# Sums of v for five blocks a visit beside the sequence transform, two exponential buffers in the projections' home, and one-pass turning of maxima

## The chip, the cores and the metric

The kernel runs on 1 core of one Trainium2 chip. The metric is the time of one execution in device microseconds; the median over the runs is compared.

## The reference

One sequence of 2048 rows of width 512 (x) goes two ways, and a gate for each row mixes the results. The inputs are float32.

```python
g = sigmoid((x * gate_w).sum(-1, keepdims=True))
# A: real part of a Fourier transform, by matrices, over the width and then over the sequence
a, b = x @ Wd_re.T, x @ Wd_im.T
y = Ws_re @ a - Ws_im @ b
# B: attention with 32 heads of width 16 in a causal window of 256
qkv = x @ wqkv
scores = q @ k.T * 16 ** -0.5;  mask = (0 <= i - j) & (i - j < 256)
o = softmax(where(mask, scores, -1e9)) @ v;  b_out = o @ wo
return g * y + (1 - g) * b_out
```

The weights wqkv and wo are scaled up by about 48 and 49, so scores are large and the maxima of the softmax are needed.

## The kernel before, in words

**Dense work.** Every dense product runs as three fp32r matmuls: each operand is split into a rounded part "hi" and the rest "lo", and hi x hi, hi x lo and lo x hi are summed in PSUM. A generator `dense()` yields behind each matmul, so that attention can be put between. It makes in this order: the projections to q and k of head group 0 together with v, then q and k of groups 1 to 3, with the imaginary part b of the width transform behind group 1 and the real part a at the end (`have.add("proj")` then marks that all projections are done), then the sequence transform: 16 blocks with cr, 16 with ci (L446, "dc", 48 matmuls a block), and, in its last blocks, the output projections `wo_block` (L669).

**Homes of the projections.** Results of q, k and part of a and b are evicted in split form into a tile "hl" (`split_psum`: ScalarE writes hi, VectorE writes lo) and sent to DRAM (qk_scr, ab_scr) by one 512 KB transfer of SP's queue. The tile hl has three buffers. Nothing uses it in the sequence transform.

**Attention.** There are 4 groups of heads with 32 blocks of 64 positions each, so 128 blocks, and 4 pairs of heads in a group. In round n, `s_pair` (L325) makes the scores of block n as a query block, VectorE adds the mask and takes the maximum (L327), and ScalarE takes the exponential and its row sum (L330); only maximum and sum are kept, in "ml". In the same round `t_pair` (L388) makes the transposed scores of block k = n - 20 as a key block, with the queries' maxima as an extra row of the operand in the ring, and ScalarE writes the exponentials into a tile "pt" (L389); GpSimd clears its corners (L394, L398). `pv` (L415) sums v times pt of one block into PSUM, with four 32-column parts of TensorE's array side by side; these are float32 matmuls, of which each makes two records. When eight blocks of 64 are complete, VectorE divides by the sums and SP stores them (o_scr).

**Visits.** `pv` is called at p = 2 of every third round, for three blocks; "pt" has four buffers. v of four blocks is loaded (`v_load`, "vr") and spread by GpSimd into "vpad" (`v_spread`, L378), two sets in turn, by rounds counted in fours.

**Maxima.** After eight blocks, `ml_rows` takes the reciprocal of the sums, turns the 128 x 64 tile of maxima and sums by a float32 matmul with a unit matrix (L337, two records), splits the maxima (L340, L341), copies the sums (L344), and sends them to m_scr and l_scr. It is called behind a visit. `m_ring` loads the maxima back into the ring by ScalarE's queue two or more rounds later.

**Order.** TensorE's order is as written (a manual schedule); `fill` puts 3 to 3.6 dense matmuls beside each pair. The other engines are ordered by a scheduler; `behind(e)` holds an instruction back until the last marked one of engine e is issued. SP's queue issues its transfers in order, so one that waits holds up those behind it. Scores and turned scores and turned maxima share four PSUM tiles.

Of the kernel before, what the change touches and what calls it, by code (L numbers as in the profile page):

```python
# [7 lines left out]
F32 = mybir.dt.float32  # L8
F32R = mybir.dt.float32r
AF = mybir.ActivationFunctionType  # L10
OP = mybir.AluOpType
# [3 lines left out]
P = 128  # L15
# [4 lines left out]
NP = 4  # L20
BQ = 64
NB = S // BQ
WIN = 320
BIG = 1e30
SCALE = 0.25
LAG = 20
# [6 lines left out]
def fnet_window_mix(ctx: ExitStack, tc: tile.TileContext, xT, x, wqk, wv, wr, wi, cr, ci, wo, gw, out):  # L33
    nc = tc.nc

    const = ctx.enter_context(tc.tile_pool(name="const", bufs=1))
    big = ctx.enter_context(tc.tile_pool(name="big", bufs=16))
    st = ctx.enter_context(tc.tile_pool(name="st", bufs=3))
# [16 lines left out]
    def ld(dst, src):  # L55
        mark("sp", nc.sync.dma_start(dst, src))

    def f(ap):
        return ap.bitcast(F32)
# [91 lines left out]
    for h in (0, 64):  # L151
# [2 lines left out]
                                base=0, channel_multiplier=-1)  # L154
        nc.gpsimd.affine_select(m, m, pattern=[[-1, WIN]], compare_op=OP.is_ge, fill=BIG,
                                base=256, channel_multiplier=1)
    ident = const.tile([P, P], F32, name="ident")
    nc.gpsimd.memset(ident, 1.0)
    nc.gpsimd.affine_select(ident, ident, pattern=[[1, P]], compare_op=OP.is_equal, fill=0.0,
                            base=0, channel_multiplier=-1)  # L160

    half = const.tile([P, 2], F32, name="half")
# [55 lines left out]
    TERMS = ((0, 0), (0, 1), (1, 0))  # L218


    def qk_evict(g, ss, i, ps):
        hl = ev.tile([P, 2, 512], F32R, name="hl", bufs=3)
        split_psum(hl[:, 0], hl[:, 1], ps, -SCALE if i == 0 else 1.0)
        ld(qk_scr[i][g][ss].rearrange("h x s -> x h s"), f(hl[:]))

# [59 lines left out]
    def ab_proj(i, sb, w, dst=None):  # L285
        ps = ps_d.tile([P, 512], F32, name="dab", tag="d")
        yield from row_proj(sb, w, ps)
        if dst is None:
            hl = ev.tile([P, 2, 512], F32R, name="hl", bufs=3)
            split_psum(hl[:, 0], hl[:, 1], ps, 1.0 if i == 0 else -1.0)  # L290
            ld(ab_scr[i][sb], f(hl[:]))
        else:
            split_psum(dst[:, 0], dst[:, 1], ps)
        yield
# [16 lines left out]
        PAD[i, n] = t  # L311

    ML = {}

    def s_pair(n, p):
        j = n % NB
        u, jj = divmod(n, 8)
        if jj == 0 and p == 0:
# [11 lines left out]
        mark("act", nc.scalar.activation(sm[:, :w], sm[:, :w], AF.Exp, bias=nm[:, c], scale=-1.0,  # L330
                                         accum_out=l[:, c]))

    def ml_rows(u):
        ml = ML.pop(u)
        nc.vector.reciprocal(ml[:, 1], ml[:, 1])
        pt = ps_a.tile([P, 512], F32, name="s", tag="st")
        nc.tensor.matmul(pt[:64, :P], ml.rearrange("p x c -> p (x c)"), ident, start=True, stop=True)  # L337
        hl = at.tile([32, 2, 2, 64], F32R, name="mhl", bufs=1)
        m = pt[:32, :P].rearrange("c (a r) -> c a r", a=2)
        nc.vector.tensor_scalar(hl[:, :, 0], m, -1.0, None, op0=OP.mult)  # L340
        nc.vector.scalar_tensor_tensor(hl[:, :, 1], m, -1.0, f(hl[:, :, 0]), op0=OP.mult, op1=OP.subtract)  # L341
        ld(m_scr[u].rearrange("x p (j r) -> (p j) x r", r=64), f(hl[:]).rearrange("c a h r -> c (a h) r"))
        lt = at.tile([64, P], F32, name="lt", bufs=1)
        nc.vector.tensor_copy(lt[32:64], pt[32:64, :P])  # L344
        for a in range(2):
            ls = l_scr[u]
            ld(bass.AP(tensor=ls.tensor, offset=ls.offset + a * 512, ap=[[1024, NP], [64, 8], [1, 64]]),
               lt[32:64, 64 * a:64 * a + 64])

    def m_ring(u):  # L350
        U = u % 4
        with behind("act"):
            nc.scalar.dma_start(f(ring[0][96:100, :, U * 512:(U + 1) * 512]), m_scr[u])

    OT = {}
    V2 = {}
    PT = {}

    VR = {}

    def v_load(n):
        if n >= NG * NB:
            return
        g, kb = divmod(n, NB)
        raw = at.tile([P, 4, 64], F32, name="vr", bufs=1)
        for h in range(2):
            ld(raw[64 * h:64 * h + 64].rearrange("r (c j) x -> r c j x", j=2),
               v_scr[kb // 4][:, :, h, g, :].rearrange("c (j r) x -> r c j x", r=64))
        VR[n] = raw

    def v_spread(n):
        if n >= NG * NB:
            return
        raw = VR.pop(n)
        v2 = vpad[n // 4 % 2]
        for h in range(2):
            r = slice(64 * h, 64 * h + 64)
            nc.gpsimd.tensor_copy(v2[r, :, :, 16 * h:16 * h + 16], raw[r].rearrange("r j (p d) -> r j p d", d=16))  # L378
        V2[n // 4] = v2

    def t_pair(n, p):
        q0 = n % NB * BQ
        w = min(WIN, S - q0)
        if p == 0:
            PT[n] = at.tile([P, NP, WIN], F32, name="pt", bufs=4)
        pt = PT[n]
        ps = ps_a.tile([P, 512], F32, name="t", tag="st")
        nc.tensor.matmul(ps[:, :w], PAD[1, n][:, p], ring[0][:, p, q0:q0 + w], start=True, stop=True)  # L388
        nc.scalar.activation(pt[:, p, :w], ps[:, :w], AF.Exp, scale=-1.0)  # L389
        if p % 2:  # L390
            ph = slice(p - 1, p + 1)
            for h in (0, 64):
                a = pt[h:h + 64, ph, 0:64]
                nc.gpsimd.affine_select(a, a, pattern=[[0, 2], [1, 64]], compare_op=OP.is_ge, fill=0.0,  # L394
                                        base=0, channel_multiplier=-1)
                if w == WIN:
                    a = pt[h:h + 64, ph, 256:320]
                    nc.gpsimd.affine_select(a, a, pattern=[[0, 2], [-1, 64]], compare_op=OP.is_gt, fill=0.0,  # L398
                                            base=0, channel_multiplier=1)

    def pv(n):
        g, kb = divmod(n, NB)
        v2 = V2[n // 4][:, n % 4]
        pt = PT.pop(n)
        q0 = kb * BQ
        w = min(WIN, S - q0)
        q = q0
        while q < q0 + w:
            sb = q // 512
            e = min(q0 + w, (sb + 1) * 512)  # L410
            first = (g, sb) not in OT
            if first:
                OT[g, sb] = ps_o.tile([P, 512], F32, name="o")
            for p in range(NP):
                nc.tensor.matmul(OT[g, sb][32 * p:32 * p + 32, q - sb * 512:e - sb * 512], v2[:, p],  # L415
                                 pt[:, p, q - q0:e - q0], start=first, stop=kb == 8 * sb + 7,
                                 skip_group_check=True)
# [260 lines left out]
    def need(key):  # L678
        while key not in have:
            next(stream)  # L680
# [22 lines left out]

    ctx.enter_context(tc.manual_schedule(engines={mybir.EngineType.PE}))
    N = NG * NB
    maxima = sent = 0
    taken = []
    need(("qk", 0, 0))
    ring_ahead(0)
    need(("v", 5))  # L710

    for n in range(N + LAG + 2):
        if n in (1, 3, 5):
            for i in range(2):
                clear_rows(1 - i, (n + 1) // 2)
        if n == 7:
            clear_pads()
        k = n - LAG
        ring_ahead(n + 1)
        if -4 <= k < N - 4 and k % 4 == 0:  # L720
            for c in range(2):
                need(("v", (k + 4) % NB // 2 + c))
            with behind(*(("sp",) if k < 4 else ())):
                v_load(k + 4)
        if -4 <= k and k % 4 == 3:
            v_spread(k + 1)
        if n == 0:
            make_pad(0, 0)
        for p in range(NP):
            if n < N:  # L730
                s_pair(n, p)
            fill(n)
            if 0 <= k < N:
                t_pair(k, p)
            if p == 0:
                make_pad(0, n + 1)
                if k >= -1:
                    make_pad(1, k + 1)
            fill(n)
            if p == 2 and sent < maxima and n >= taken[sent] + 2:  # L740
                m_ring(sent)
                sent += 1
            if p == 2 and k % 3 == 0:
                for j in range(k - 3, k):
                    if 0 <= j < N:
                        pv(j)
                if maxima < 16 and n > 8 * maxima + 8:
                    ml_rows(maxima)
                    maxima += 1
                    taken.append(n)  # L750
    attention_done()
    for _ in stream:
        pass
# [44 lines left out]
```

## Time and profile before

| | us |
|---|---|
| median of 3 runs | 869.55 |
| lowest and highest | 868.85, 870.48 |
| the profiled execution | 873.39 |
| its span | 871.3 |

The page of the profile gives busy time by engine (PE is TensorE's matmuls, PEld its loading of weights, DVE VectorE, ACT ScalarE, POOL GpSimd, SP the queue of transfers), the span in 40 slices, the chain that ended last, and the costliest groups of instructions. A row of a timeline gives the start and the duration in us, the engine, the line, the operation, the tiles written and read, the shape and the count; in brackets stands idle time before it and what ended it. The end of a matmul is modelled, so starts are the surer reading.

### The profile page before, as it was taken

The page shows a single profiled execution, that of the slowest core. Times are in us where ns is not written, and L with a number is a line of the kernel's source. Part 1 is how long each engine was busy: PE and PEld are TensorE (multiplying, and loading weights), DVE is VectorE, ACT ScalarE, POOL GpSimd, SP SyncE. Part 2 cuts the span into 40 slices and gives each one's busy share as a digit, 9 for nine tenths or more (in the row PEclk, how much of TensorE's full clock was granted, in tenths as well). Part 3 has the DMA queues.
Part 4 walks back from the last instruction along what each step waited for, and adds up shares of the span by engine and source line. Part 5 has one row for each costly group of instructions (what it writes and reads, how often), then busy time and mean ns, then how long its engine had stood idle before and what let it go on. Part 6 is the DMA issues. An engine that isn't in the chain of part 4 may idle for free.

```text
span 871.3 us, 17146 instructions
## 1 busy us (share of the span) xinstructions
PE 860.5 (99%) x5160; PEld 690.3 (79%) x5160; DVE 611.3 (70%) x1974; ACT 580.9 (67%) x1793; POOL 384.6 (44%) x1067
## 2 busy tenths in 40 slices
PE   8999999999999999999999999999999999999998
PEld 6888778787877778878788887878778787788886
DVE  4588987667878987878787777788876444564431
ACT  4388799888897987878788777877776454111110
POOL 9100054545444756656456566554546665200000
PEclk9999999999999999999999999999999999999999
DMA  6875796464749436644445354599944333485541
GB/s 229 266 226 155 248 262 197 153 214 158 241 158 289 130 105 225 172 130 135 134 131 170 105 163 133 156 349 256 329 148 159 123 118 114 130 263 192 189 145 48
DMA packets 93132, 157.87 MB, mean 181 GB/s; under 512 B 27120, under 2 KB 36080, under 8 KB 93040
## 3 DMA queue, kind: packets, MB, share of 16 engines
q1 hardware_dynamic: 92288, 155.61, 56.5%
q10 hardware_dynamic: 752, 1.18, 0.4%
q8 instruction: 40, 0.66, 0.3%
q14 instruction: 52, 0.43, 0.2%
HBM read 106.69 MB, written 50.07 MB: 180 GB/s over the span
## 4 chain that ended last, share of the span: by engine, by line
PE 92%; DVE 3%; DMA 2%; ACT 1%; issue 1%; SPq 0%; DVEq 0%; ACTq 0%
PE dc L446 40%; PE dab L266 9%; PE s L325 8%; PE o L415 8%; PE dqk L244 8%; PE t L388 8%; PE t L669 5%; PE dv L266 4%; DVE sm L327 1%; PE s L232 1%; DMA raw<-x 1%; ACT sm L330 1%; DMA ring<-qk_scr 1%; PE s L337 1%; DMA pt<-xT 0%
## 5 line engine op out<-in xcount | busy, mean ns | idle before, releaser
L446 PE MATMUL dc<-big,hi 128*128 128x512 f32 x1024 | 355.4, 395 | 0.0
L394 POOL TENSOR_SCALAR_AFFINE_SELECT pt<-pt 64x128 f32<-64x128 f32 x512 | 191.9, 375 | 276.4 <-ACT pt L389 261.2
L330 ACT ACTIVATE sm<-sm,ml 128x320 f32<-128x320 f32 (+4 forms) x512 | 277.3, 543 | 49.4 <-DVE ml L327 48.0
L327 DVE CUSTOM_DVE_ANT_0 sm<-s,mask 128x320 f32<-128x320 f32 (+4 forms) x512 | 230.7, 462 | 82.7 <-PE s L325 62.5
L389 ACT ACTIVATE pt<-t 128x320 f32<-128x320 f32 (+4 forms) x512 | 208.7, 412 | 89.8 <-PE t L388 86.2
L446 PEld LDWEIGHTS dc<-big,hi 128*128 128x128 f32 x1024 | 186.3, 188 | 32.6 <-issue 2.4
L446 PE MATMUL dc<-big,lo 128*128 128x512 f32 x512 | 201.6, 394 | 0.0
L398 POOL TENSOR_SCALAR_AFFINE_SELECT pt<-pt 64x128 f32<-64x128 f32 x448 | 161.9, 361 | 0.1
L325 PE MATMUL s<-ring,pad 128*128 128x320 f32 (+4 forms) x512 | 159.0, 310 | 0.9 <-DVE ml L327 0.5
L388 PE MATMUL t<-ring,pad 128*128 128x320 f32 (+4 forms) x512 | 155.1, 303 | 1.6 <-DVE ml L327 0.9
L310 DVE TENSOR_SCALAR pad<-ring,half 96x256 fp32r<-96x256 f32 x384 | 121.6, 358 | 24.2 <-PE t L388 22.0
L325 PEld LDWEIGHTS s<-ring,pad 128*128 128x128 f32 x512 | 96.0, 188 | 36.6 <-issue 7.4
L388 PEld LDWEIGHTS t<-ring,pad 128*128 128x128 f32 x512 | 96.1, 188 | 21.6 <-DVE ml L327 2.6
L446 PEld LDWEIGHTS dc<-big,lo 128*128 128x128 f32 x512 | 96.3, 188 | 10.6
L81 DVE TENSOR_TENSOR lo<-raw,hi 128x512 fp32r<-128x512 f32 x146 | 99.6, 712 | 1.4 <-PE dc L446 1.3
L330 ACT ACTIVATION_READ_ACCUMULATOR sm<-sm,ml 128x1 f32 x512 | 98.8, 193 | 0.0
L266 PE MATMUL dab<-hi,big 128*128 128x512 f32 x256 | 90.9, 396 | 0.0
L244 PE MATMUL dqk<-big,hi 128*128 128x512 f32 x240 | 86.7, 394 | 0.6 <-DVE hl L86 0.5
L80 DVE CAST hi<-raw 128x512 fp32r<-128x512 f32 x142 | 58.6, 453 | 38.3 <-PE dc L446 37.1
L415 PE MATMUL o<-pt,vpad 128*32 128x320 f32 (+4 forms) x1408 | 73.8, 351 | 0.0
L378 POOL COPY vpad<-vr 64x256 f32<-64x256 f32 x64 | 26.0, 405 | 91.1 <-DMA vr<-v_scr 72.0
L308 ACT ACTIVATE pad<-ring,half 96x256 fp32r<-96x256 f32 x128 | 64.1, 500 | 0.0
(82 smaller groups left out, 780.3 us busy)
## 6 DMA issues: line engine op xcount, KB each, us to landing
qk_scr<-hl SPq DMA_DIRECT2D x32, 512.0 KB
ring<-qk_scr SPq DMA_DIRECT2D x32, 512.0 KB
raw<-cr SPq DMA_DIRECT2D x32, 512.0 KB
raw<-ci SPq DMA_DIRECT2D x32, 512.0 KB
ab_scr<-hl SPq DMA_DIRECT2D x20, 512.0 KB
big<-ab_scr SPq DMA_DIRECT2D x20, 512.0 KB
r_scr<-ev SPq DMA_DIRECT2D x36, 256.0 KB
ev<-r_scr SPq DMA_DIRECT2D x36, 256.0 KB
```

Of the source, the lines that this page charges most:

```text
L244: nc.tensor.matmul(ps, w[a][:, c:c + 128], XT[dk, ss][:, b], start=n == 0, stop=n == 11)
L266: nc.tensor.matmul(ps, XT[dk, ss][:, a, c * 128:(c + 1) * 128], wh[b], start=n == 0, stop=n == 11)
L310: nc.vector.tensor_scalar(dst, src, half[:96, h:h + 1], None, op0=OP.mult)
L325: nc.tensor.matmul(ps[:, :w], PAD[0, n][:, p], ring[1][:, p, k0:k0 + w], start=True, stop=True)
L327: mark("dve", nc.vector.tensor_tensor_reduce(out=sm[:, :w], in0=ps[:, :w], in1=mask[:, WIN - w:], scale=1.0, scalar=3e38, op0=OP.add, op1= ...
L330: mark("act", nc.scalar.activation(sm[:, :w], sm[:, :w], AF.Exp, bias=nm[:, c], scale=-1.0, accum_out=l[:, c]))
L388: nc.tensor.matmul(ps[:, :w], PAD[1, n][:, p], ring[0][:, p, q0:q0 + w], start=True, stop=True)
L389: nc.scalar.activation(pt[:, p, :w], ps[:, :w], AF.Exp, scale=-1.0)
L394: nc.gpsimd.affine_select(a, a, pattern=[[0, 2], [1, 64]], compare_op=OP.is_ge, fill=0.0, base=0, channel_multiplier=-1)
L398: nc.gpsimd.affine_select(a, a, pattern=[[0, 2], [-1, 64]], compare_op=OP.is_gt, fill=0.0, base=0, channel_multiplier=1)
L415: nc.tensor.matmul(OT[g, sb][32 * p:32 * p + 32, q - sb * 512:e - sb * 512], v2[:, p], pt[:, p, q - q0:e - q0], start=first, stop=kb == 8 ...
L446: nc.tensor.matmul(ps, w[a][:, i % 8 * 128:i % 8 * 128 + 128], ab[SC[i]][:, b], start=i == ends[0] and a + b == 0, stop=i == ends[1] and a ...
```

## The change

It does four things.

- `pv` is called when three blocks wait, and, once all projections are done, when five wait; v is loaded and spread by what has been summed, not by rounds.
- "hl" gets two buffers instead of three, each of the size of a "pt" tile. Once the projections are done, two of every six exponential tiles are put there, so that there are six.
- The maxima are turned in two steps: `ml_split` splits maxima and reciprocals on VectorE, `ml_turn` turns both halves by one-pass fp32r matmuls two rounds later, and `ml_rows` adds the halves of the sums. Their rounds are fixed (`TURN`), and they no longer stand behind a visit.
- The loop has one round less.

```diff
+    def hl_tile():
+        t = ev.tile([P, NP, WIN], F32R, name="hl", bufs=2)
+        return t.rearrange("p a b -> p (a b)")[:, :1024].rearrange("p (h s) -> p h s", h=2)
...
-        hl = ev.tile([P, 2, 512], F32R, name="hl", bufs=3)
+        hl = hl_tile()
...
+    def ml_split(u):
+        ml = ML.pop(u).rearrange("p x c -> p (x c)")
+        MH[u] = at.tile([P, 2, NP * 16], F32R, name="mlh", bufs=1)
+        with behind("dve"):
+            nc.vector.reciprocal(ml[:, 32:], ml[:, 32:])
+            nc.vector.tensor_copy(MH[u][:, 0], ml)
+            mark("dve", nc.vector.tensor_sub(MH[u][:, 1], ml, f(MH[u][:, 0])))
+
+    def ml_turn(u):
+        hl = MH.pop(u)
+        MT[u] = ps_a.tile([P, 512], F32, name="s", tag="st")
+        for h in range(2):
+            nc.tensor.matmul(MT[u][:64, h * P:h * P + P], hl[:, h], ident, start=True, stop=True)
+
     def ml_rows(u):
-        ml = ML.pop(u)
-        nc.vector.reciprocal(ml[:, 1], ml[:, 1])
-        pt = ps_a.tile([P, 512], F32, name="s", tag="st")
-        nc.tensor.matmul(pt[:64, :P], ml.rearrange("p x c -> p (x c)"), ident, start=True, stop=True)
-        hl = at.tile([32, 2, 2, 64], F32R, name="mhl", bufs=1)
-        m = pt[:32, :P].rearrange("c (a r) -> c a r", a=2)
-        nc.vector.tensor_scalar(hl[:, :, 0], m, -1.0, None, op0=OP.mult)
-        nc.vector.scalar_tensor_tensor(hl[:, :, 1], m, -1.0, f(hl[:, :, 0]), op0=OP.mult, op1=OP.subtract)
+        pt = MT.pop(u)
+        rows = at.tile([64, 2 * P], F32R, name="mhl", bufs=1)
+        hl = rows[:32].rearrange("c (a h r) -> c a h r", a=2, h=2)
+        lt = f(rows[32:64, :P])
+        m = pt[:32, :2 * P].rearrange("c (h a r) -> c h a r", h=2, a=2)
+        with behind("dve"):
+            nc.vector.tensor_scalar(hl.rearrange("c a h r -> c h a r"), m, -1.0, None, op0=OP.mult)
+            nc.vector.tensor_copy(lt, pt[32:64, :P])
+            mark("dve", nc.vector.tensor_add(lt, pt[32:64, P:2 * P], lt))
...
-            PT[n] = at.tile([P, NP, WIN], F32, name="pt", bufs=4)
+            if "proj" in have:
+                more.append(n)
+            if more and (n - more[0]) % 6 < 2:
+                PT[n] = f(ev.tile([P, NP, WIN], F32R, name="hl", bufs=2)[:])
+            else:
+                PT[n] = at.tile([P, NP, WIN], F32, name="pt", bufs=4)
...
+    TURN = (8, 1, ml_split), (10, 0, ml_turn), (10, 1, ml_rows), (13, 0, m_ring)
...
-    for n in range(N + LAG + 2):
+    for n in range(N + LAG + 1):
...
-            if p == 2 and sent < maxima and n >= taken[sent] + 2:
-                m_ring(sent)
-                sent += 1
-            if p == 2 and k % 3 == 0:
-                for j in range(k - 3, k):
-                    if 0 <= j < N:
-                        pv(j)
-                if maxima < 16 and n > 8 * maxima + 8:
-                    ml_rows(maxima)
-                    maxima += 1
-                    taken.append(n)
+            for at_n, at_p, do in TURN:
+                u, j = divmod(n - at_n, 8)
+                if p == at_p and j == 0 and 0 <= u < 16:
+                    do(u)
+            if p == 2 and (k - summed >= (5 if more else 3) or k == N):
+                for j in range(summed, k):
+                    pv(j)
+                summed = k
+                while 4 * spread - 5 < summed and 4 * spread < N:
+                    v_spread(4 * spread)
+                    spread += 1
+                    v_next(4 * spread)
```

The unit matrix "ident" becomes fp32r.

More of the change, by code (lines that the diff above doesn't have):

```diff
@@ L156, in fnet_window_mix @@
                                 base=256, channel_multiplier=1)
-    ident = const.tile([P, P], F32, name="ident")
-    nc.gpsimd.memset(ident, 1.0)
-    nc.gpsimd.affine_select(ident, ident, pattern=[[1, P]], compare_op=OP.is_equal, fill=0.0,
+    ident = const.tile([P, P], F32R, name="ident")
+    nc.gpsimd.memset(f(ident[:]), 1.0)
+    nc.gpsimd.affine_select(ident[:], f(ident[:]), pattern=[[1, P]], compare_op=OP.is_equal, fill=0.0,
                             base=0, channel_multiplier=-1)
@@ L288, in ab_proj @@
         if dst is None:
-            hl = ev.tile([P, 2, 512], F32R, name="hl", bufs=3)
+            hl = hl_tile()
             split_psum(hl[:, 0], hl[:, 1], ps, 1.0 if i == 0 else -1.0)
@@ L313, in fnet_window_mix @@
     ML = {}
+    MH = {}
+    MT = {}
     def s_pair(n, p):
@@ L331, in s_pair @@
                                          accum_out=l[:, c]))
-    def ml_rows(u):
-        ml = ML.pop(u)
-        nc.vector.reciprocal(ml[:, 1], ml[:, 1])
-        pt = ps_a.tile([P, 512], F32, name="s", tag="st")
-        nc.tensor.matmul(pt[:64, :P], ml.rearrange("p x c -> p (x c)"), ident, start=True, stop=True)
-        hl = at.tile([32, 2, 2, 64], F32R, name="mhl", bufs=1)
-        m = pt[:32, :P].rearrange("c (a r) -> c a r", a=2)
-        nc.vector.tensor_scalar(hl[:, :, 0], m, -1.0, None, op0=OP.mult)
-        nc.vector.scalar_tensor_tensor(hl[:, :, 1], m, -1.0, f(hl[:, :, 0]), op0=OP.mult, op1=OP.subtract)
-        ld(m_scr[u].rearrange("x p (j r) -> (p j) x r", r=64), f(hl[:]).rearrange("c a h r -> c (a h) r"))
-        lt = at.tile([64, P], F32, name="lt", bufs=1)
-        nc.vector.tensor_copy(lt[32:64], pt[32:64, :P])
+    def ml_split(u):
[10 more added lines that the diff above has]
+            nc.tensor.matmul(MT[u][:64, h * P:h * P + P], hl[:, h], ident, start=True, stop=True)
+    def ml_rows(u):
+        pt = MT.pop(u)
[7 more added lines that the diff above has]
+            mark("dve", nc.vector.tensor_add(lt, pt[32:64, P:2 * P], lt))
+        ld(m_scr[u].rearrange("x p (j r) -> (p j) x r", r=64), f(hl).rearrange("c a h r -> c (a h) r"))
         for a in range(2):
@@ L347, in ml_rows @@
             ld(bass.AP(tensor=ls.tensor, offset=ls.offset + a * 512, ap=[[1024, NP], [64, 8], [1, 64]]),
-               lt[32:64, 64 * a:64 * a + 64])
+               lt[:, 64 * a:64 * a + 64])
     def m_ring(u):
@@ L357, in fnet_window_mix @@
     PT = {}
+    more = []
     VR = {}
@@ L705, in fnet_window_mix @@
     N = NG * NB
-    maxima = sent = 0
-    taken = []
+    TURN = (8, 1, ml_split), (10, 0, ml_turn), (10, 1, ml_rows), (13, 0, m_ring)
     need(("qk", 0, 0))
@@ L710, in fnet_window_mix, with v_next @@
     need(("v", 5))
-    for n in range(N + LAG + 2):
+    summed, spread = 0, 2
+    def v_next(n):
+        if n < N:
+            for c in range(2):
+                need(("v", n % NB // 2 + c))
+            with behind(*(("sp",) if n < 8 else ())):
+                v_load(n)
+    for n in range(N + LAG + 1):
         if n in (1, 3, 5):
@@ L719, in fnet_window_mix @@
         ring_ahead(n + 1)
[L720 to L725, printed above, removed]
+        if k in (-4, 0):
+            v_next(k + 4)
+        if k in (-1, 3):
             v_spread(k + 1)
+        if k == 3:
+            v_next(8)
         if n == 0:
```

## The prediction

> **What bounds the kernel now.** I read the page first (busy times, slices, chain), then TensorE's timeline around the sums of v and the turnings, then the queues and ScalarE around the evictions of the projections.
>
> ```profile
> PE 860.5 (99%) x5160; PEld 690.3 (79%) x5160; DVE 611.3 (70%) x1974; ACT 580.9 (67%) x1793; POOL 384.6 (44%) x1067
> PE   8999999999999999999999999999999999999998
> PEclk9999999999999999999999999999999999999999
> PE 92%; DVE 3%; DMA 2%; ACT 1%; issue 1%; SPq 0%; DVEq 0%; ACTq 0%
> ```
>
> TensorE is busy in every slice, at full granted clock, and carries 92% of the chain that ended last. So two things can move the time: TensorE's own work, and new stalls of TensorE. The idle time of the other engines is cover, not a gain.
>
> **Part 1: fewer visits to the sums of v.** One visit, with what stands before and behind it on TensorE (columns: start, duration, line, form, count):
>
> ```profile
> 524.00 0.40 PE L446 MATMUL dc<-big,lo 128*128 128x512 f32 x1
> 524.32 1.83 PE L415 MATMUL o<-pt,vpad 128*32 128x128 f32 x40
> 526.09 0.41 PE L325 MATMUL s<-ring,pad 128*128 128x320 f32 x1
> 526.34 0.40 PE L446 MATMUL dc<-big,hi 128*128 128x512 f32 x1
> 526.57 0.30 PE L388 MATMUL t<-ring,pad 128*128 128x320 f32 x1
> 526.72 0.40 PE L446 MATMUL dc<-big,hi 128*128 128x512 f32 x1
> ...
> 758.84 21.12 PE dc L446 x92
> ```
>
> Durations overlap, so I take differences of starts. An undisturbed 512-wide matmul costs 21.12/92 = 0.23. Before the visit it costs 0.32 (524.00 to 524.32), so 0.09 is lost going in. The visit runs 1.77 (to 526.09). The 320-wide score matmul behind it takes 0.25, while a 320-wide one inside the stream, at 526.57, hands on after 0.15; so 0.10 is lost coming out. How much of the 1.77 is fixed comes from the last, short visit:
>
> ```profile
> 757.99 0.39 PE L446 MATMUL dc<-big,hi 128*128 128x512 f32 x1
> 758.30 0.54 PE L415 MATMUL o<-pt,vpad 128*32 128x128 f32 x16
> 758.77 0.50 PE L446 MATMUL dc<-big,hi 128*128 128x512 f32 x1
> ```
>
> That one sums 192 columns (128 and 64, the last two blocks) in 0.47; the other sums 3 blocks of 320, 960 columns, in 1.77. So a column costs 1.30/768 = 1.69 ns, and 0.47 - 192 x 1.69 ns = 0.15 is fixed. A visit therefore costs 0.09 + 0.15 + 0.10 = 0.34 beyond its columns, whatever it sums.
>
> Visits before: k = 3, 6, ... 129, which is 43. In the changed kernel's order of TensorE instructions there are 14 visits of three blocks (to k = 42), then k = 47, 52, ... 127 and a last one at 128: 14 + 18 = 32. The columns stay. So 11 x 0.34 = **-3.7 us**, all on TensorE and so on the path.
>
> **Part 2: turning the maxima.** Before, 14 of the 16 turnings stand directly behind a visit and two stand alone. A lone one, then one behind a visit:
>
> ```profile
> 96.73 0.39 PE L244 MATMUL dqk<-big,hi 128*128 128x512 f32 x1
> 97.05 0.43 PE L337 MATMUL s<-ident,ml 128*64 128x128 f32 x2
> 97.41 0.41 PE L325 MATMUL s<-ring,pad 128*128 128x320 f32 x1
> 97.66 0.39 PE L244 MATMUL dqk<-big,hi 128*128 128x512 f32 x1
> ...
> 555.16 1.84 PE L415 MATMUL o<-pt,vpad 128*32 128x256 f32 x48
> 556.93 0.43 PE L337 MATMUL s<-ident,ml 128*64 128x128 f32 x2
> 557.29 0.41 PE L325 MATMUL s<-ring,pad 128*128 128x320 f32 x1
> 557.54 0.39 PE L446 MATMUL dc<-big,lo 128*128 128x512 f32 x1
> ...
> 341.45 0.33 PE L325 MATMUL s<-ring,pad 128*128 128x128 f32 x1
> 341.62 0.68 PE L446 MATMUL dc<-big,hi 128*128 128x512 f32 x2
> ```
>
> The lone one costs 0.09 going in, 0.36, and 0.10 coming out: 0.55. Behind a visit it adds only 0.36, since the way out is paid anyway. Before: 14 x 0.36 + 2 x 0.55 = 6.1. In the changed order all 16 turnings stand alone, two blocks after their split, as two one-pass fp32r matmuls of 128 columns. No such turning is in the trace. The nearest rows are the score matmuls, also fp32r: directly behind a switch the 128-wide one takes 0.17 (341.45), the 320-wide 0.25 (557.29), so 0.08/192 = 0.42 ns a column, 0.05 for 128 columns, 0.11 for two. With 0.09, 0.15 and 0.10 for the switches that is about 0.44 each, 7.0 in all: **+0.9 us**. So the cheaper matmul is more than eaten by losing the shared way out. The ends: switches alone, 0.34 x 16 = 5.4 (-0.7), and as dear as today's lone one, 8.8 (+2.7).
>
> VectorE gets six small operations a turning instead of four, so 2 x 16 x 0.28 = 9 us by the 0.28 of today's copy; at 70% busy that is covered. It loses a wait:
>
> ```profile
> DVE mhl L340 <- PE s L337: 24.8, 16, 2.7
> ```
>
> Before, VectorE stood 24.8 us at L340 until the visit and the turning behind it were through; now it meets the turning one pair later, with the score matmul in between, and needs no wait. TensorE shows hardly any wait on it, so I count 0 for both (bounds -0.5 and +0.5, as VectorE is full around 105 us, see below). The split is issued behind the scores of the block after the last of the eight, when ScalarE has summed them. m_scr and l_scr move a few places up in SP's queue, past evictions and ring loads, by a few us; nobody waits for them (m_ring comes three blocks later).
>
> **Part 3: two buffers "hl" instead of three.** ScalarE writes an eviction into hl, VectorE the rest, and SP sends 512 KB. With two, ScalarE's eviction j + 2 waits until the send of j has landed, and every exponential queues behind it on ScalarE; then PSUM tiles stay taken and TensorE stands. Before, no such wait is there. The room that two buffers would leave is read from rows of ScalarE and of SP; the two tightest in the loaded stretch:
>
> ```profile
> 88.27 0.57 ACT L84 ACTIVATE hl<-dqk 128x512 fp32r<-128x512 f32 x1
> 94.76 0.58 ACT L84 ACTIVATE hl<-dqk 128x512 fp32r<-128x512 f32 x1
> 98.31 0.60 ACT L84 ACTIVATE hl<-dqk 128x512 fp32r<-128x512 f32 x1 [0.49 <-PE dqk L244]
> 104.93 0.60 ACT L84 ACTIVATE hl<-dqk 128x512 fp32r<-128x512 f32 x1 [1.07 <-PE dqk L244]
> ...
> 90.75 0.37 SPq L56 DMA_DIRECT2D qk_scr<-hl  x1
> ...
> 101.07 0.40 SPq L56 DMA_DIRECT2D qk_scr<-hl  x1
> ```
>
> The eviction of 88.27 is sent at 90.75, and the next but one begins at 94.76: 4.0 us. That of 98.31 is sent at 101.07 and the next but one begins at 104.93: 3.9. How long the send takes is bounded by two rows:
>
> ```profile
> 761.91 0.33 SPq L56 DMA_DIRECT2D o_scr<-ev  x1
> ...
> 764.87 1.48 SPq L56 DMA_DIRECT2D ev<-o_scr  x3
> ...
> 82.18 5.97 DMA ring<-qk_scr
> ```
>
> A store of half the size has landed 2.96 after its issue (the load that needs it goes at 764.87). A ring load, the last of four in a row, took 5.97. And the stretch is full:
>
> ```profile
> 80.00:90.00 10.00, 10.00 (x50) 8.59 (x49) 8.27 (x33) 8.07 (x26) 0.00 (x0) 1.00 0.82 228
> 90.00:100.00 10.00, 9.94 (x48) 7.80 (x47) 9.28 (x38) 8.35 (x27) 0.79 (x2) 1.00 0.74 241
> 100.00:110.00 10.00, 9.43 (x43) 7.03 (x42) 10.00 (x36) 7.46 (x24) 1.07 (x3) 1.00 0.72 229
> 110.00:120.00 10.00, 9.82 (x50) 8.24 (x49) 8.64 (x32) 10.00 (x33) 3.90 (x11) 1.00 1.05 235
> ```
>
> (Columns: window, length, PE, PEld, DVE, ACT, POOL busy, clock, DMA share, GB/s.) VectorE is busy 10.00 of 10 in one of these windows, ScalarE in the next, and TensorE loses 0.8 us here already. I take 4.5 us for the send, between the ends and nearer the store: 0.5 and 0.6 of wait at the two places, few others, most of it passed on because these engines are full: **+0.8 us**. The low end is 0 (landing below 3.9). At the high end, 6 us, the two places wait 2 each and some six more with 4.6 to 5.6 of room wait 0.4 to 1.4 each: 8 to 9 on ScalarE, of which about 1 us a time is buffered in PSUM for the mildest; some +5 on TensorE. The page "DMA: Bandwidth & Descriptors" of the Trainium skill (section "Anatomy of one DMA", given for GpSimd's path) puts a transfer at about 2.0 us plus its bytes over 436 GB/s; as an estimate 3.2 us for 512 KB, with which Part 3 would cost nothing and the sum be -2.8. The 2.96 seen here for half the size fits it; the 5.97 does not.
>
> **Part 4: longer visits, more buffers, the end.** A visit of five keeps TensorE from scores for 2.9 us instead of 1.8; ScalarE must keep up in the longer stretches between. It does, by its row for 336 to 660 us:
>
> ```profile
> L389 ACT ACTIVATE pt<-t 128x320 f32<-128x320 f32 (+4 forms) x251 | 102.2, 409 | 26.9 <-PE t L388 26.1
> ```
>
> It still stands idle 26 us there for the next matmul, so no backlog would grow over five blocks: 0 (if that cover were gone, about 1 us for each of 18 visits). Six exponential buffers for five waiting blocks leave the same single spare as four for three. GpSimd's spreads wait for a visit as before, a stretch ahead of their use. At the end, 59 dense matmuls (13.5 us) instead of 92 (21.1) lie between the last sum and the first output projection; its first three blocks use o_scr of sums finished at earlier visits, and the cast of the prepared rows ran well ahead:
>
> ```profile
> 769.21 0.62 ACT L78 CAST os<-ev 128x512 fp32r<-128x512 f32 x1 [16.80 <-DMA ev<-o_scr]
> ```
>
> That is 10.4 after the last visit (758.77), inside 13.5: 0, at worst +1.
>
> **The sum.** -3.7 + 0.9 + 0.8 = -2.0 us on a span of 871.3, in an execution of 873.39. The median shown is 869.55 (868.85 to 870.48), so 867.55, rounded 867.6.
>
> **Rivals.** *Sends land late (slower).* If a 512 KB store takes 6 us in the full stretches, as the 5.97 speaks for, Part 3 costs 5: -3.7 + 0.9 + 5 = +2.2, 871.8. It decides from about 5 us of landing upwards. The page "Trainium Kernel Development and Optimization" of the Trainium skill (section "Key Constraints") says that all queues' transfers run on the same 16 DMA engines and interleave, which makes this likelier where the DMA share is 1.05. Against: only a stretch of some 30 us is that full. *The turning gains nothing.* If fp32r turnings cost today's lone 0.55, then -3.7 + 2.7 + 0.8 = -0.2, 869.4, no change. For it speaks that excursions from the full array grow in number, from 45 to 48. *Two buffers are enough.* -3.7 + 0.9 = -2.8, 866.8, as no wait on a send exists today.
>
> **How the numbers follow.** About 0.2% (1.7 us) can be told from no change. Forecast 0.46 (0.36 faster, 0.10 just short of the mark), two buffers enough 0.12, turning gains nothing 0.22, late sends 0.20. Faster 0.48, same 0.32, slower 0.20. Range: low by -3.7 and -0.7, 865.2; high by the late sends, 872.0.
>
> **What would show it.** In the profile after: 32 runs of sums; 0.44 from switch to switch at each turning; the wait at mhl gone; "ACT hl <- DMA" of about 1 us in total; 18 visits of 2.9 us without scores waiting behind. It is wrong if ScalarE's waits on sends exceed 4 us, if TensorE's idle time in 60 to 280 us grows by more than 2, or if TensorE stands at the first output projection.

## The result, and the profile after

| | before | after |
|---|---|---|
| median of 14 runs, us | 870.48 | 877.33 |
| lowest and highest | 868.85, 876.13 | 872.78, 881.42 |
| the profiled execution | 873.39 | 873.27 |
| its span | 871.3 | 871.2 |

The changed kernel is slower: the ratio is 1.0063, 95% interval 1.0048 to 1.0077, about 5.5 us (the two medians by themselves differ by 6.9). The prediction said 867.6, with 872.0 as its upper end.

The two profiled executions look alike only because that of before began late. TensorE's timeline of before and then of after, the first score matmul of each:

```profile
37.01 0.19 PE L325 MATMUL s<-ring,pad 128*128 128x64 f32 x1
...
33.78 0.19 PE L331 MATMUL s<-ring,pad 128*128 128x64 f32 x1
```

From there to its end the changed kernel takes 3.1 us longer (871.2 - 33.78 against 871.3 - 37.01). The profiled execution of after is the second fastest of its 14 runs, so the trace shows less of the loss than the ratio does. The page of after: busy times, TensorE's slices, the clock, the chain.

```profile
PE 857.0 (98%) x5160; PEld 689.4 (79%) x5160; DVE 619.0 (71%) x2006; ACT 579.6 (67%) x1793; POOL 374.9 (43%) x1067
PE   9999989999999999999999999999999999999998
PE 89%; DMA 5%; DVE 4%; ACT 1%; issue 1%; SPq 0%; ACTq 0%; DVEq 0%
```

TensorE was busy 860.5 and is now 857.0. But one slice is no longer full (the sixth, 109 to 131 us), and transfers carry 5% of the chain instead of 2%. The chain in order of time names them (start, duration; the four longest):

```profile
111.09 8.25 DMA qk_scr<-hl
270.76 8.61 DMA raw<-x
572.73 11.04 DMA raw<-ci
600.32 8.77 DMA raw<-ci
```

The first of these is the new wait. ScalarE's evictions, then TensorE's timeline:

```profile
106.85 0.58 ACT L84 ACTIVATE hl<-dqk 128x512 fp32r<-128x512 f32 x1
111.18 0.59 ACT L84 ACTIVATE hl<-dqk 128x512 fp32r<-128x512 f32 x1
119.36 0.60 ACT L84 ACTIVATE hl<-dab 128x512 fp32r<-128x512 f32 x1 [3.18 <-DMA qk_scr<-hl]
...
117.61 0.31 PE L413 MATMUL t<-ring,pad 128*128 128x320 f32 x1
120.74 0.69 PE L270 MATMUL dab<-hi,big 128*128 128x512 f32 x1 [2.82 <-DVE hl L88]
121.23 0.63 PE L270 MATMUL dab<-lo,big 128*128 128x512 f32 x1
...
123.60 2.14 PE L440 MATMUL o<-pt,vpad 128*32 128x320 f32 x24
125.67 0.41 PE L331 MATMUL s<-ring,pad 128*128 128x320 f32 x1
```

A send of 512 KB goes at 111.09 and lands 8.25 later. The next but one eviction has waited for it 3.18 on ScalarE, VectorE's half comes behind, and TensorE, with both PSUM tiles of the projections taken, stands until 120.74: 3.13 from 117.61, of which the matmul there takes 0.15, so 2.98 is lost. Then it is slow as well: the matmuls at 121.23 and behind it hand on after 0.43 instead of 0.23 (121.23 to 121.66), and the visit takes 2.07 instead of 1.75 to 1.77. The windows say why (columns as in the prediction):

```profile
110.00:120.00 10.00, 7.91 (x40) 6.46 (x38) 6.22 (x26) 6.82 (x23) 4.12 (x14) 1.00 1.04 273
120.00:130.00 10.00, 9.26 (x53) 6.48 (x54) 7.22 (x21) 7.56 (x24) 4.41 (x13) 0.83 0.44 161
```

The granted clock is 0.83 behind the stall. Other waits (engine, line, for whom: us in total, times, longest):

```profile
DVE hi L80 <- DMA raw<-ci: 6.4, 5, 3.2
ACT hl L84 <- DMA qk_scr<-hl: 3.5, 2, 3.2
ACT hl L84 <- DMA ab_scr<-hl: 0.5, 1, 0.5
PE dab L270 <- DVE hl L88: 2.8, 1, 2.8
```

VectorE's wait on raw<-ci was 1.0 before. The two parts that were to save time do save it on TensorE. A turning, and a visit of five:

```profile
94.27 0.39 PE L248 MATMUL dqk<-big,hi 128*128 128x512 f32 x1
94.50 0.28 PE L351 MATMUL s<-ident,mlh 128*64 128x128 f32 x2
94.62 0.36 PE L331 MATMUL s<-ring,pad 128*128 128x320 f32 x1
94.82 0.39 PE L248 MATMUL dqk<-big,hi 128*128 128x512 f32 x1
...
553.52 0.62 PE L471 MATMUL dc<-big,hi 128*128 128x512 f32 x2
554.07 1.83 PE L440 MATMUL o<-pt,vpad 128*32 128x320 f32 x32
555.71 1.27 PE L440 MATMUL o<-hl,vpad 128*32 128x192 f32 x32
556.91 0.41 PE L331 MATMUL s<-ring,pad 128*128 128x320 f32 x1
557.16 0.39 PE L471 MATMUL dc<-big,lo 128*128 128x512 f32 x1
```

The visit takes 2.84 for 1600 columns, 0.09 going in and 0.10 coming out, as forecast. The turning takes 0.12 for both matmuls, nothing going in (0.23 from 94.27 to 94.50) and 0.05 coming out.

### The profile page after: what moved, and what is told of

Its sections match the earlier page's. It is cut to its first block, busy times and chain, and to the rows that moved or that the text cites. A ratio compares the mean times of both kernels' runs of the same rounds, so it can differ in the third digit from the quotient of the medians.

```text
span 871.2 us, 17180 instructions
## 1 busy us (share of the span) xinstructions
PE 857.0 (98%) x5160; PEld 689.4 (79%) x5160; DVE 619.0 (71%) x2006; ACT 579.6 (67%) x1793; POOL 374.9 (43%) x1067
## 4 chain that ended last, share of the span: by engine, by line
PE 89%; DMA 5%; DVE 4%; ACT 1%; issue 1%; SPq 0%; ACTq 0%; DVEq 0%
PE dc L471 38%; PE dqk L248 9%; PE dab L270 8%; PE s L331 8%; PE t L413 8%; PE o L440 7%; PE dv L270 5%; PE t L694 5%; DMA raw<-ci 2%; DMA raw<-x 1%; DMA qk_scr<-hl 1%; DVE lo L81 1%; DVE sm L333 1%; ACT sm L336 1%; DVE pad L314 1%
## 5 line engine op out<-in xcount | busy, mean ns | idle before, releaser
L419 POOL TENSOR_SCALAR_AFFINE_SELECT pt<-pt 64x128 f32<-64x128 f32 x396 | 142.1, 359 | 223.7 <-ACT pt L414 211.9
L414 ACT ACTIVATE pt<-t 128x320 f32<-128x320 f32 (+4 forms) x396 | 160.4, 412 | 42.3 <-PE t L413 41.5
L423 POOL TENSOR_SCALAR_AFFINE_SELECT pt<-pt 64x128 f32<-64x128 f32 x348 | 121.4, 349 | 0.1
L419 POOL TENSOR_SCALAR_AFFINE_SELECT hl<-hl 64x128 f32<-64x128 f32 x116 | 43.7, 377 | 55.7 <-ACT hl L414 52.0
```

## Experiments

Times are medians. "Ratio" is to the kernel before on the same chip (870.3 to 870.9 in every set of runs), with its 95% interval. Theory: two homes make a late send block ScalarE. Rivals: the longer visits, or the order of the turning, cost it.

### One part at a time

**Three homes in the changed kernel.**

```diff
+    homes = const.tile([P, 3 * 1024], F32R, name="homes")
+    sent = iter(range(999))
     def hl_tile():
-        t = ev.tile([P, NP, WIN], F32R, name="hl", bufs=2)
-        return t.rearrange("p a b -> p (a b)")[:, :1024].rearrange("p (h s) -> p h s", h=2)
+        c = next(sent) % 3 * 1024
+        return homes[:, c:c + 1024].rearrange("p (h s) -> p h s", h=2)
...
-                PT[n] = f(ev.tile([P, NP, WIN], F32R, name="hl", bufs=2)[:])
+                c = (n - more[0]) % 6 * NP * WIN
+                PT[n] = f(homes[:, c:c + NP * WIN]).rearrange("p (a b) -> p a b", a=NP)
```

> The changed kernel, but the projections keep three homes of 512 KB each for their evictions (one region of 12 KB a partition, in which the two extra exponential tiles lie once the projections are done). Theory L (a late send: with two homes ScalarE waits at 119 us for a send of 8 us, TensorE stands 3 us and its clock falls): the stall and the low clock go; what is left is the gain of 11 visits (3.7) and of the turnings (16 x 0.17 instead of 6.1: 3.4), so 863 to 865 against some 870.5 of the kernel before. Theory V (the longer visits starve ScalarE and VectorE, stalls at 550 to 650 us): the time stays at 870 or above, whatever the homes are.

Measured: 871.45, ratio 1.0009 (0.9995 to 1.0024). The stall at 117 is gone, but there is no gain over the kernel before, where 863 to 865 was expected: a second loss is left.

**Two homes in the kernel before** (`bufs=3` of "hl" becomes `bufs=2`).

> The kernel before, with two homes instead of three for the projections' evictions and nothing else changed. Theory L: slower by the stall and the lost clock, 3 to 10 us, 874 to 880 with a spread of several us, and a row of ScalarE's hl waiting for a send. Theory V: no change, 870.5 within 1.

Measured: 873.7, ratio 1.0037 (1.002 to 1.0053). Two homes alone cost some 3 us, just under the 874 to 880 expected, with a stall of 2.15 at 119.14; no lower clock follows it in this trace.

**The new turning in the kernel before** (the three functions and their rounds; three homes, visits of three; v is loaded by what has been summed, as in the changed kernel).

> The changed kernel with three homes of the old size, and with visits of three blocks to the end (so four exponential tiles): the new turning alone, with v loaded by what is summed. By the trace after, a turning costs 0.12 and 0.05 coming out: -3.4, so 867 for theories L and V alike. Theory T (the turnings by themselves, or the earlier sends of the maxima, make the loss): 872 or above. By the price of the prediction (0.44 each): 871.4.

Measured: 871.14, ratio 1.001 (0.9998 to 1.0022). TensorE has less to do, and no time is won. In this trace the first visit takes 3.16 instead of 1.75: it waits for GpSimd, whose spread of v waits for its load ahead of the corner clears. This is not the turning's alone: in two other traces whose program is that of the kernel before up to there, the first visit takes 2.45 and 2.47. TensorE, then GpSimd, in this run:

```profile
119.83 1.81 PE L437 MATMUL o<-pt,vpad 128*32 128x320 f32 x20
122.33 0.73 PE L437 MATMUL o<-pt,vpad 128*32 128x320 f32 x4 [0.69 <-POOL pt L420]
...
117.62 0.39 POOL L397 COPY vpad<-vr 64x256 f32<-64x256 f32 x1 [6.02 <-DMA vr<-v_scr]
```

**The changed kernel with visits of three** (`more.append(n)` taken out).

> The changed kernel with visits of three blocks to the end; homes (two) and turning as changed. Theory L: the stall comes before the sequence transform, so it stays, and 11 visits come back: 3.7 slower than the changed kernel, some 880. Theory V: the loss goes, 867.

Measured: 875.06, ratio 1.0044 (1.0029 to 1.006). So the longer visits, as they stand in the changed kernel, do not save the 3.7: with them it is 0.0019, 1.7 us, slower, with about 1.8 either way, which can't be told from no change. That is between the two expectations and called for a second theory: what TensorE saves is given back in stretches where the DMA engines are full.

### The full stretch

From about 555 to 630 us sixteen loads of 512 KB bring b for the second half of the sequence transform. They were left out in both kernels; the second half reads a's tiles again, so b is missing from the result:

```diff
         def next_b():
             sc = todo_b.pop(0)
-            with behind("sp"):
-                nxt[sc] = load_ab(1, sc)
...
-        ab = nxt
```

> The kernel before, but the second half of the sequence transform reads a's tiles again, so that the 16 loads of 512 KB that bring b between about 550 and 630 us are gone (this leaves b out of the result). Theory "full stretch": what the changed kernel saves on TensorE is given back where the DMA engines are full, because VectorE's split of the next ci piece waits in order for its load. The kernel before loses little there (its waits of VectorE on raw<-ci sum to 1.0 us), so it gains at most 1.5: 868.8 to 870.3. Rival "visits" (a visit of five, not the transfers, makes scores late): 870.3, no change.

> The changed kernel with three homes (as in the first experiment), and without the loads of b, as in the run beside it. Theory "full stretch": the stalls of TensorE between 582 and 612 us (0.74, 0.68, 2.99, 0.40 in the run with three homes) and the lower clock behind them go, and it is 4 to 6 us faster than the run without loads of b of the kernel before: 864.5 to 866. Rival "visits": the stalls stay, 870.5 to 871.5.

Measured: the kernel before 869.37, ratio 0.9988 (0.9975 to 1.0001); the changed one with three homes 865.85, ratio 0.9946 (0.9932 to 0.996). Without these loads the change wins 0.0042, 3.7 us with about 1.7 either way, over the kernel before treated alike; with them it wins nothing. The second loss hangs on this stretch.

### Two waits side by side

In the run with three homes TensorE stands at 605.63. TensorE's, VectorE's and ScalarE's rows there:

```profile
605.63 0.39 PE L475 MATMUL dc<-big,lo 128*128 128x512 f32 x1
608.85 0.63 PE L334 MATMUL s<-ring,pad 128*128 128x320 f32 x1 [2.84 <-ACT homes L418]
...
607.21 0.76 DVE L80 CAST hi<-raw 128x512 fp32r<-128x512 f32 x2 [4.76 <-DMA raw<-ci]
...
607.14 0.64 ACTq L375 DMA_DIRECT2D ring<-m_scr  x1
607.82 0.56 ACT L339 ACTIVATE sm<-sm,ml 128x320 f32<-128x320 f32 x1 [5.85 <-DVE hi L80]
```

VectorE waits in order for a piece of ci, with the maxima behind it. ScalarE waits at the same time, with the issue of m_ring in its queue. The profiled execution of the changed kernel itself has no such single stop here: from the visit at 579.53 to that at 633.43 it takes 53.9, this run 57.0 (575.33 to 632.31), and the two runs with all the edits that follow 51.1 and 52.1, with the same work on TensorE. So its loss here, 1.8 to 2.8 in that execution, comes in pieces of under 0.8.

**Each piece of cr and ci loaded one piece earlier than it is split.** The second run also puts the first spread of v behind the corner clears.

```diff
         def get(k):
-            for _ in range(2 if k not in w else 1):
-                if todo:
-                    cc, j = todo.pop(0)
-                    w[cc, j] = load_split((cr, ci)[cc][j // 2, j % 2])
+            n = 2 - len(w)
+            while len(PEND) < n + len(ahead) and todo:
+                cc, j = todo.pop(0)
+                PEND.append((w, (cc, j), load_raw((cr, ci)[cc][j // 2, j % 2])))
+            for _ in range(n):
+                if PEND:
+                    cut()
+            ahead[:] = [1]
             return w.pop(k)
```

> The changed kernel with three homes, and each piece of cr and ci is loaded one piece earlier than it is split (same two raw buffers, the same bytes at about the same times). Theory "full stretch": VectorE's waits on raw<-ci (10.9 us in the run with three homes) fall below 2, the stall of 2.99 at 605 us goes, 866.5 to 868.5. Rival "the loads only trade places": the ring's or r_scr's loads come later instead and stall as long, 870 to 871.5. Rival "visits": VectorE's waits go and TensorE stalls all the same, 870.5 to 871.5.

> As the run beside it, and GpSimd's first spread of v's second set stands behind the corner clears of the first visit instead of ahead of them, so that the first visit doesn't wait for vr. Theory: the first visit takes 1.76 instead of 2.9 to 3.2 us, another -1.2 against the run beside it: 865.3 to 867.3. Rival (the visit then waits for vpad or the clears all the same, or the next visit does): no change against the run beside it.

Measured: 874.37, ratio 1.0037 (1.0023 to 1.0051), and 873.41, ratio 1.0031 (1.0022 to 1.0041). Both miss what was expected, by 6 us. VectorE's waits on raw<-ci fell from 10.9 to 2.8, but TensorE's stall grew: TensorE, ScalarE and the chain of the first of the two.

```profile
610.62 0.64 PE L334 MATMUL s<-ring,pad 128*128 128x320 f32 x1 [6.15 <-ACT homes L418]
...
608.90 0.64 ACTq L375 DMA_DIRECT2D ring<-m_scr  x1
609.59 0.56 ACT L339 ACTIVATE sm<-sm,ml 128x320 f32<-128x320 f32 x1 [9.18 <-DMA ring<-qk_scr]
...
595.76 13.12 DMA ring<-qk_scr
```

The ring's load was issued at 595.76 and landed 13.12 later, at 608.88; m_ring goes at 608.90. So m_ring on ScalarE's queue waits for the ring's load, and every exponential behind it waits too.

**m_ring earlier** (`(13, 0, m_ring)` becomes `(11, 3, m_ring)`, ahead of that load): with three homes alone, with the early pieces and late spread as well, and in the changed kernel with its two homes. Beside them the kernel before with m_ring late:

```diff
-            if p == 2 and sent < maxima and n >= taken[sent] + 2:
+            if p == 0 and sent < maxima and n >= 8 * sent + 13:
```

> The changed kernel with three homes, and m_ring (the load of the maxima into the ring, on ScalarE's queue) two places earlier in the program: round 11, p = 3 instead of round 13, p = 0. Theory "order": in round 13 it stands behind the ring's own load of round 12, waits on ScalarE's queue until that has landed (13.1 us after issue in the run with early pieces), and every exponential behind it waits as well. Ahead of that load it needs only m_scr, 5 to 8 us old: ScalarE's waits at 600 to 610 us, the stall of TensorE of 2.99 at 605 us and the lower clock behind it go, 866.5 to 868.5. Rival "pieces": VectorE's wait of 4.8 us on raw<-ci in the same place stalls TensorE all the same, 870.5 to 871.5.

> As the run beside it, with pieces of cr and ci loaded one piece earlier and the first spread of v behind the clears of the first visit. Theory "order": without m_ring in the way the early pieces are a gain, not a loss as in the run that had them alone (874.4): 865.5 to 867.5. Rival: the earlier pieces push the ring's loads later and cost more than they give, 869 to 872.

> The kernel before with m_ring in the changed kernel's place (round 13 of its eight blocks, p = 0) and nothing else. Theory "order": it now waits for the ring's load there, and the kernel before loses what the changed one loses in the full stretch: 872.5 to 875.5. Rival "pieces" (m_ring's place is harmless, the loss comes from TensorE being ahead of its pieces): 870 to 871.

> The changed kernel with its two homes and m_ring in round 11, p = 3. Theory "order": the part of the loss that is not the homes' goes, 877.3 less 2 to 4: 873 to 875.5; the stall at about 118 us stays with the lower clock behind it. Rival: the homes are the whole loss, 877.

Measured: 873.27, ratio 1.0024 (1.0008 to 1.0039); 868.12, ratio 0.9972 (0.9959 to 0.9985); 871.27, ratio 1.0002 (0.9993 to 1.0011); 876.45, ratio 1.0073 (1.0059 to 1.0087). Neither edit helps alone, and m_ring's place does no harm to the kernel before, where 872.5 or more was expected of it. With m_ring early the other wait remains (VectorE, then TensorE, in the first of these runs):

```profile
611.40 0.76 DVE L80 CAST hi<-raw 128x512 fp32r<-128x512 f32 x2 [5.74 <-DMA raw<-ci]
...
613.22 0.63 PE L334 MATMUL s<-ring,pad 128*128 128x320 f32 x1 [2.96 <-DVE ml L336]
```

With both away TensorE runs through, while the stretch is as full as ever; a window of the run that has both edits:

```profile
600.00:610.00 10.00, 10.00 (x82) 7.85 (x81) 8.52 (x29) 6.92 (x24) 6.21 (x17) 1.00 1.04 259
```

This run has the late spread as well. Between the two runs with early pieces above it made 0.0006, which can't be told from nothing, and with the early m_ring it was not tried apart.

### The faster version, and each part against it

"All fixes" is three homes, early m_ring, early pieces and late spread. First the early pieces in the kernel before; then all fixes with visits of three; with two homes; and again as it is.

> The kernel before with the pieces of cr and ci loaded one piece earlier, and nothing else. Its waits of VectorE on raw<-ci sum to 1.0 us, so there is little to win: 869.5 to 870.8. Rival: the earlier pieces are the gain of the faster version (868.1 against 870.5) and the change's parts bring nothing: 868 to 868.5.

> The faster version (three homes, early m_ring, early pieces, late first spread), but with visits of three to the end. If the visits of five are worth their 11 x 0.34 once nothing waits, it loses 2.5 to 3.7 against the faster version: 870.6 to 871.8. Rival (what a longer visit saves is lost in scores that come late, so that only the turning is worth anything): 867.5 to 868.5.

> The faster version, but with the changed kernel's two homes in place of three. If the homes cost what they cost alone in the kernel before (873.7 against 870.3), it loses 3 to 6 against the faster version, with a stall of 2 to 4 us at 118 us: 871.5 to 874. Rival (with the order mended the sends land in time too): 868.

> The faster version again, as the reference of the three runs beside it: 867.5 to 869, ratio to the kernel before 0.996 to 0.9985.

| run | median, us | ratio |
|---|---|---|
| before with early pieces | 872.09 | 1.0012 (1.0001 to 1.0023) |
| all fixes, visits of three | 873.05 | 1.0022 (1.0009 to 1.0035) |
| all fixes, two homes | 872.94 | 1.0028 (1.0011 to 1.0044) |
| all fixes | 867.53 | 0.997 (0.9958 to 0.9982) |

The early pieces are no gain by themselves. Against all fixes, visits of three lose 0.0052 (4.5 us) and two homes lose 0.0058 (5.0 us). All fixes beat both kernels, twice. What the longer visits are worth on TensorE can be read where nothing stalls. In both forms a visit ends with 57 blocks summed and another with 87, and between them lie the same thirty blocks, scores and turnings, with six visits of five (the first run of all fixes) or ten of three. The score matmul behind each of these two visits, in the two runs:

```profile
401.93 0.41 PE L334 MATMUL s<-ring,pad 128*128 128x320 f32 x1
554.08 0.41 PE L334 MATMUL s<-ring,pad 128*128 128x320 f32 x1
...
399.96 0.41 PE L334 MATMUL s<-ring,pad 128*128 128x320 f32 x1
553.38 0.41 PE L334 MATMUL s<-ring,pad 128*128 128x320 f32 x1
```

That is 152.15 against 153.42: 1.27 for four visits, 0.32 each.

With two homes the stall at 118 is back, the send of the same eviction and the same clock (ScalarE; the window):

```profile
120.31 0.60 ACT L84 ACTIVATE hl<-dab 128x512 fp32r<-128x512 f32 x1 [3.48 <-DMA qk_scr<-hl]
...
120.00:130.00 10.00, 8.32 (x48) 5.67 (x49) 6.29 (x18) 7.25 (x22) 5.13 (x14) 0.83 0.50 184
```

## Why the prediction was wrong

**The size of Part 3, the homes.** The mechanism was named, and the rival "sends land late" has the right sign. What was mis-sized is the landing: 4.5 us taken, 6 as the high end, 8.25 measured. The prediction put the send between a store of 2.96 and a ring load of 5.97 and took a value nearer the store; the ring load, from the full stretch, was the nearer row, and still too early in it. The page "DMA: Bandwidth & Descriptors" of the Trainium skill (section "Anatomy of one DMA", given there for GpSimd's path, while this send goes by SP's queue) leads to 3.2 us as an estimate, and the 8.25 does not agree with it. The place was missed as well: the two tightest rooms hardly wait (ScalarE waits three times, 4.0 us in all, 3.2 of it at once); the wait fell on a room of 5.1 (from the issue at 111.09 to 116.18, when ScalarE was ready: 119.36 less 3.18), because the landing there was long: the send issued at 86.17, for which ScalarE waited 0.36 until 90.86, took 4.7, near the 4.5 of the prediction. The term is +5.0 (two homes against three, all fixes; about 1.8 either way) instead of +0.8, the end that the prediction gave as its worst. And it priced TensorE's idle time alone: the lower clock behind a stall was not in the sum.

**Part 2's last sentence.** "nobody waits for them (m_ring comes three blocks later)" failed. m_ring is not waited for, but it waits itself, for the ring's load that now stands ahead of it, and it does so at the head of ScalarE's queue. This and VectorE's wait on raw<-ci make the second loss: from three homes alone (1.0009) to all fixes (about 0.997) it is 0.0038, some 3.3 us, the late spread included.

**Part 1, the visits.** Right on TensorE (0.09, 0.10, 2.84 against 2.9; 0.32 for each visit saved against 0.34, so 3.5 for eleven). In time it is -4.5 with an interval of about 1.5 either way, which holds the -3.7; but only where the waits are gone. In the changed kernel as it stands it brings nothing.

**Part 2, the turning.** The term of 0.44 each was mis-sized the other way. The way in costs nothing, and each turning takes 0.12 and 0.05. The 0.36 of before was not the price of the 64-column form. What is left of it can be seen from the third group of heads to the fourth (the first score matmul of each, 64 columns wide): with visits of three and the new turning (all fixes, visits of three) 164.42, in the kernel before 164.92, so 0.13 for each of four turnings, about 2 us in all. In time it brought nothing that could be told: 1.001 alone, and 1.0022 against 1.0012 beside all fixes and early pieces. That 1.001 is about the +0.9 of the prediction is luck, as its price of a turning was wrong. Where these 2 us go in each run is not settled: in the run with the turning alone the first visit's wait and a stall of 1.26 at 277.61 come in between, but traces with the old turning show waits of this kind too (1.25 at 278.04, kernel before with early pieces). Visits of three, then the kernel before:

```profile
328.22 0.19 PE L334 MATMUL s<-ring,pad 128*128 128x64 f32 x1
492.64 0.19 PE L334 MATMUL s<-ring,pad 128*128 128x64 f32 x1
...
331.62 0.19 PE L325 MATMUL s<-ring,pad 128*128 128x64 f32 x1
496.54 0.19 PE L325 MATMUL s<-ring,pad 128*128 128x64 f32 x1
```

**Part 4, the longer visits.** Its 0 for the end held: the changed kernel's last 59 dense matmuls end at 769.11, and its first output projection begins at 769.12. Its 0 for the stretches between visits agrees with the 0.32 a visit where nothing stalls; in the full stretch the two waits named above come in.

**The sum, with what was measured.** All fixes -2.6 (0.997), two homes +5.0, order and pieces +3.3: +5.7, against 5.5 (1.0063), if the parts add up. The prediction's -2.0 is near the first of these, but by luck: that one holds no two homes, and it is -4.5 for the visits and +1.9 for the rest (1.0022). What it left out is that waits which the profile of before hardly shows grow when TensorE arrives earlier and the transfers no sooner.

**What would have shown it.** TensorE's idle time in 60 to 280 and ScalarE's waits on sends were named as marks. The first showed it: it grew from 1.8 to 4.9, more than the 2 allowed. The second, 4.0 us in all, stood at the mark of 4 and did not exceed it, and yet cost more than it showed.

## What to carry to other kernels

When an edit saves time on the engine that bounds a kernel, look at what arrives just in time in the full stretches: the engine will be there earlier, and in-order queues (a load's issue on ScalarE, a split on VectorE) turn a late transfer into a stall of everything behind it. Two such waits in one place hide each other: taking away either one gains nothing or loses, so test them together before dropping either. Price a buffer that is taken away by the landing times of the fullest stretch, and a stall of a few microseconds on TensorE with the slower clock behind it.

## What was not expected of the hardware

**The clock falls behind stalls of under 3 us, sometimes.** A stall of 2.98 us was followed by 0.83 in the next 10 us, and matmuls of 0.43 for some 2.3 us; stalls of 2.15 (two homes in the kernel before) and of 2.63 (at 276, with three homes and early m_ring alone) were not. Over the traces of all these runs, behind the first 20 us and by TensorE's idle time in brackets (about 0.2 less than the loss): each of the eight stalls of 2.82 to 6.15 was followed by a window with a clock of 0.66 to 0.92, and none of 2.46 or less was. In between, 2.55 (changed kernel with early m_ring, at 283.68) and 2.58 (below) were, and 2.62 (changed kernel with visits of three, at 120.86) was not. The stall that all fixes leave at about 276, VectorE waiting for raw<-x with the maxima behind it, shows both. TensorE and the window in the second of its runs:

```profile
275.93 0.39 PE L273 MATMUL dab<-hi,big 128*128 128x512 f32 x1
278.90 0.41 PE L417 MATMUL t<-ring,pad 128*128 128x320 f32 x1 [2.58 <-DVE ml L336]
...
280.00:290.00 10.00, 10.00 (x43) 8.61 (x44) 9.13 (x33) 9.00 (x28) 6.22 (x18) 0.83 0.45 142
```

That execution took 870.24. In the profiled execution of the first run the same stall was 1.97, the clock stayed at 1.00 there, and it took 866.32; the stall is one part of that difference. The page "TensorE: Matmul & The Clock Gate" of the Trainium skill (section "What's actually happening") says that the clock halves after an idle window of about 3.4 us and that the window runs freely. The halved rate agrees (0.43 for 0.23); the 2.98, and the idle times of 2.55 and 2.58, are below the window that it names, so by that length alone the clock would not have fallen. That the window runs freely could be why 2.55 was followed by a lower clock and 2.62 was not. It would also make the same stall cost more in one run than in another, and the 14 runs of the changed kernel do spread with the clock: 872.78 to 873.95 at 0.998, 881.42 at 0.992. That this is the reason was not tested. One trace of a kernel with two homes took nearly as long, 879.40 (early m_ring), and has three stalls, 3.81, 2.55 and 3.17, with a lower clock behind each.

**The way into and out of a narrower array is not one price.** The float32 turning of 64 columns cost 0.09 going in and 0.36; the fp32r one of 64 columns costs nothing going in. Whether it is the type or the 32-column parts that makes the sums of v pay 0.09 and 0.10 was not tried.
